# Pooled q, k and v of the first batch summed by TensorE from the blocks' own tiles, with four weight pieces loaded first

## The chip, the cores and the metric

The kernel runs on one core of a Trainium2 chip. The metric is the device time of one execution in microseconds (us); lower is better. The core has TensorE (PE, matrix products), VectorE (DVE), ScalarE (ACT), GpSimd (POOL) and SyncE (SP, which here issues nearly all transfers). PEld is TensorE's loading of the stationary operand.

## The reference

Three layers are computed one after the other. q, k and v are float32 in the shape (batch 4, heads 8, positions 576, depth 64).

```python
def _attn_ref(q, k, v):
    q_d, k_d, v_d = (t.reshape(B, H, 144, 4, D).mean(axis=3) for t in (q, k, v))
    out_up = np.repeat(softmax(q_d @ k_d.T / 8) @ v_d, 4, axis=2)   # pooled attention
    mask = np.abs(pos[:, None] - pos[None, :]) < 4                  # local attention
    out_local = softmax(where(mask, q @ k.T / 8, -1e9)) @ v
    return out_up + out_local            # then as x: 2304 tokens x 512

def _moe_ref(x, w_in, w_out):            # 512 -> 2048 -> 512
    h = x @ w_in
    return (h * np.cos(h)) @ w_out

def _moe2_ref(x, w_gate, w_val, w_out, rms_g):   # 512 -> 1536 -> 512
    xn = x / sqrt(mean(x * x) + 1e-6) * rms_g
    g = xn @ w_gate
    return (silu(g) * (xn @ w_val)) @ w_out
```

## The kernel before, in words

**An order that a planner writes.** The kernel is not written in the order in which it runs. Each piece of work is a Python generator that asks for an engine and a planned duration (`yield "PE", 0.44`), for a buffer (`take`) or for an event (`wait`). The class `Order` steps through them with planned clocks of the engines and emits each instruction to its engine in that planned order. Among pieces that could start within 0.1 us of each other it prefers the one with the earlier due time, weighted by `WD`. Once emitted, each engine runs its own list strictly in order: an instruction that waits holds up all that stand behind it. Where the plan sees PE idle, `keep_warm` puts in products of the identity matrix that nobody uses, named `warm` (line 251).

**The stages.** Attention of a batch has a pooled and a local part. The pooled part needs q and k summed over groups of four positions and transposed (`trq`, line 425 for the first batch), copied into `pqs`; then scores `sps` (line 539), exponentials `E` (line 550), transposes `tra` (line 575), products with pooled v `avp` (line 594), and the result `od` (line 602). The local part goes in five blocks u0 to u4 of about 116 positions: a tile `raw` of 128 positions of q and of k for all heads, transposes `btr` (line 646), scores `bs` (line 690) in a band, exponentials `bE`, transposes `bat` (line 726), products with v `bav` (line 752, with v in `vb`). A block then adds `od` (line 762, DVE), and line 775 (ACT) and line 777 (POOL) split it in two parts into `big`, the input of the first dense layer. That layer works on 256 tokens at a time: `h` (line 1013), cosine (lines 1031 to 1049), `y` (line 1079). The second layer (`gvp`, line 1502, and `o`, line 1755) follows after all of this. The first `h` needs the blocks u0 to u2 of the first batch with their pooled part, and the first weights.

**Weights** come as pieces of 512 KB in a 64-bit format (`raww`), and ACT, DVE and POOL make two TensorE operands of each (lines 316 to 327).

**Before, the start** is made of these transfers, all issued by SP: q and k of the first batch in a layout with the four positions of a group side by side (`pq`, 2.4 MB), with v's blocks (`vb`) in between, four weight pieces, q and k of block u0 once more as `raw`, v in a pooled layout (`v4`, 16 transfers), the blocks u1 to u4. DVE sums q (line 385), POOL sums k (lines 380 and 382) and v (lines 504 to 511).

Of the kernel before, what the change touches and what calls it, by code (L numbers as in the profile page):

```python
# [9 lines left out]
F32 = mybir.dt.float32  # L10
# [37 lines left out]
TP = 5  # L48
WD = 0.005
NQS = 1  # L50
CVB, GLB = 9, 0.5
T0, T1, U1, U2 = 70, 52, 6.5, 4.26
DU = {"conv": 20, "pool": -320, "blk": -200}


class Order:
# [20 lines left out]
    def give(self, name, item, t=None):  # L77
        self.pools.setdefault(name, []).append((self.now() if t is None else t, item))
# [114 lines left out]
def fused_kernel(ctx: ExitStack, tc, q, k, v, w_in, w_out, w_gate, w_val, w_out2, rms_g, mask, bmask, out):  # L193
# [86 lines left out]
    def w_loads(m, pieces, src):  # L280

        for i in pieces:
            S_.due(conv_due(m, i) - 5.0)
            r = yield take("raw")
            p = yield take(PLACES, 1)
# [90 lines left out]
    def sum4(b, w, t, o, n):  # L376

        if b or w:
            yield "POOL", 0.05 + n * 0.32
            POOL.tensor_tensor(out=t[:, :n, 0:2], in0=t[:, :n, 0:2], in1=t[:, :n, 2:4], op=ALU.add)  # L380
            yield "POOL", 0.05 + n * 0.18
            POOL.tensor_tensor(out=o, in0=t[:, :n, 0], in1=t[:, :n, 1], op=ALU.add)
        else:
            yield "DVE", 0.05 + n * 0.27
            DVE.tensor_reduce(out=o, in_=t[:, :n].rearrange("p u r d -> p u d r"), axis=AX.X, op=ALU.add)

# [26 lines left out]

    def pq_first(w, c, t, qs, place):

        u0, n = UC[c]
        yield wait(("pq", w, c))
        yield from sum4(0, w, t, qs[:, u0:u0 + n], n)
        give("pqp", place)
        yield take("att")  # L420
        i = yield take("bank")
        ps = bank_tile(i, [64, 4, 128], "trq")
        yield "PE", 0.2 * n
        for x in range(n):
            PE.transpose(ps[:, x, :], qs[:, u0 + x, :], ident)
        yield from pq_ev(0, w, c, ps)
        give("bank", i)
        give("att", "att")
        count(("pq", 0), 6)

# [55 lines left out]

    def pv(b, hp, t=None, place=None, vh=None):

        vi = 0
        if b == 0:  # L490
            yield wait(("pv", hp))
        else:
            vi = yield take("vh")
            vh = VH[vi]
            p = []
            for _ in range(2):
                x = yield take("pq")
                p.append(x)
            t = (ap.tile([128, 512], F32, tag=p[0], name="v4").rearrange("p (c x) -> p c x", c=2),
                 ap.tile([128, 512], F32, tag=p[1], name="v4")[:, :256])  # L500
            yield from pv_load(b, hp, *t)
# [10 lines left out]
        if b == 0:  # L512
            give(place[2], place)
        else:
            for x in p:
                give("pq", x)
        vd[b, hp] = (vh, vi)
        done(("v", b, hp))

    def pooled(b, hp, E=None):  # L520
# [109 lines left out]
    def block(b, u, raw, pools):  # L630
# [9 lines left out]
        for w in range(2):  # L640
# [4 lines left out]
            for a in range(4):  # L645
                PE.transpose(t[:, a, :], raw[w][:, 2 * a:2 * a + 2].rearrange("t h d -> t (h d)"), ident)  # L646
            if pools[w]:
                give(*pools[w])
# [104 lines left out]
        give("b2", a_i)  # L753
        give("vb", v_i)
        t0 = (S_.cur["t"], "PE")
# [38 lines left out]
    def raw_dma(t, src, b, u):  # L794

        r0 = geo(u)[2]
        yield "SP", 0.73
        SP.dma_start(t, src[b, :, r0:r0 + 128, :].rearrange("h t d -> t h d"))

    VI = {}  # L800

    def block_v():

        for b in range(B):
            for u in range(5):
                S_.due(blk_due(b, u) - 5.0)
                x = yield take("vb")
                VI[b, u] = x
                r0 = geo(u)[2]
                vp = v[b].rearrange("(a e) t d -> e t a d", e=2)  # L810
                for s, (_, _, kc) in enumerate(groups(u)):
                    for e in range(2):
                        yield "SP", 0.5
                        SP.dma_start(VB[x][64 * e:64 * e + 64, s], vp[e, r0 + kc:r0 + kc + 64])
                done(("rv", b, u))

# [25 lines left out]
    def start():  # L842

        pl = {}
        pq_tiles(0)
        for n in [("pq", w, c) for c in range(3) for w in range(2)] + [("qs", w) for w in range(2)] + [("E", hp) for hp in (1, 2, 3)] \
                + [("v4", hp) for hp in range(4)] + [("vhl", 0)] + [("raw", u) for u in range(5)]:
            pl[n] = yield take(PLACES)
# [3 lines left out]

        def load(ev, us):
            yield "SP", us

        qs = [early(("qs", w), [128, 9, 64]) for w in range(2)]
        for c, (u0, n) in enumerate(UC):
            for w in range(2):
                t = early(("pq", w, c), [128, 4, 4, 64])
                yield "SP", max(0.48, 0.37 * n)  # L860
                SP.dma_start(t[:, :n], pq_src(0, w, u0, n))
                done(("pq", w, c))
                S_.add(pq_first(w, c, t, qs[w], pl["pq", w, c]), 0.0, S_.now())
        E = EP + [early(("E", hp), [72, 2, 3, 2, 64]) for hp in (1, 2, 3)]
# [4 lines left out]
        for hp in range(4):  # L869
            S_.add(pooled(0, hp, E[hp]), 0.0)  # L870
        vh0 = early(("vhl", 0), [128, 2, 3, 128])
        vh0 = VH + [vh0[:, 0], vh0[:, 1]]
        for x in vh0:
            yield "POOL", 0.5
            POOL.memset(x, 0.0)
# [12 lines left out]

        def values0():
            for hp in range(4):  # L890
                t = early(("v4", hp), [128, 768])
                t = t[:, :512].rearrange("p (c x) -> p c x", c=2), t[:, 512:]
                yield from pv_load(0, hp, *t)
                done(("pv", hp))
                S_.add(pv(0, hp, t, pl["v4", hp], vh0[hp]), 0.0, S_.now())

# [5 lines left out]

        def raws(us):
            for u in us:
                t = early(("raw", u), [128, 2, 8, 64])
                for w in range(2):
                    yield from raw_dma(t[:, w], (q, k)[w], 0, u)
                done(("raw", 0, u))
                S_.add(block(0, u, (t[:, 0], t[:, 1]), (None, (pl["raw", u][2], pl["raw", u]))), blk_due(0, u))

        first = 0
        for what, n in LOADS:
            if what == "r":
                yield from raws(range(first, first + n))
                first += n
            elif what == "w":
                yield from words(n)
            else:
                yield from values0()
        yield "SP", 0.96  # L920
# [4 lines left out]

        S_.add(after("vhl", None, pl["vhl", 0]), 0.0)
        S_.add(after(("pq", 0), None, pl["qs", 0], pl["qs", 1]), 0.0)
# [5 lines left out]
        yield wait(("E2", 2))  # L933
        for _ in range(3):
            p = yield take("pqp")
            give(p[2], p)

# [910 lines left out]
```

## Time and profile before

| | us |
|---|---|
| median of 3 runs (lowest, highest) | 983.98 (982.58, 985.17) |
| the profiled execution: its time | 984.96 |
| the profiled execution: its span in the trace | 983.1 |
| outside the span | 1.86 |
| first `h` product starts at | 69.87 |
| last stretch, from 200 us to the end | 783.10 |

The span is the time from the first to the last instruction that the profiler saw; the device time of the same execution is 1.86 us longer. TensorE's granted clock is full in all 40 slices of the page.

### The profile page before, as it was taken

To read this page: it belongs to the slowest core of one execution; us is meant where nothing else is said; L and a number is where in the kernel's file an instruction comes from. 1 tells how busy PE (TensorE), PEld (TensorE's weight loads), DVE (VectorE), ACT (ScalarE), POOL (GpSimd) and SP (SyncE) were. 2 spreads that over 40 slices of the span, in tenths; PEclk is the share of its full clock that TensorE was granted. 3 is DMA by queue.
4 is the path that set the end of the run, shared out by engine and by line. 5 is a ranking of instruction groups with operands and counts; after the bars stand their busy time and mean duration, and the time that the engine had idled before them with its cause. 6 is when DMAs were issued, how large, how long until landed. Compare 5 with 4: busy or idle time off the path is not lost.

```text
span 983.1 us, 19205 instructions
## 1 busy us (share of the span) xinstructions
PE 953.0 (97%) x7150; PEld 880.4 (90%) x7150; DVE 721.2 (73%) x1460; ACT 542.3 (55%) x1090; POOL 269.1 (27%) x325
## 2 busy tenths in 40 slices
PE   6789899999999999999999999999999999999998
PEld 6688778888988888888888889999999999999998
DVE  2789976677657775666577699586666688999895
ACT  3658886677677965656566465242322334554442
POOL 3877685544336311101042242000000014300000
PEclk9999999999999999999999999999999999999999
DMA  8788643567685554544331311133222144454432
GB/s 241 212 211 246 181 147 111 148 199 180 199 231 166 170 171 128 176 144 169 120 129 65 107 44 49 49 106 93 75 82 71 57 145 132 132 174 139 141 119 76
DMA packets 160333, 136.07 MB, mean 138 GB/s; under 512 B 72176, under 2 KB 133744, under 8 KB 160240
## 3 DMA queue, kind: packets, MB, share of 16 engines
q1 hardware_dynamic: 160240, 134.85, 45.8%
q8 instruction: 56, 0.92, 0.4%
q14 instruction: 37, 0.30, 0.1%
HBM read 98.64 MB, written 36.18 MB: 137 GB/s over the span
## 4 chain that ended last, share of the span: by engine, by line
PE 84%; DMA 4%; DVE 3%; SPq 3%; issue 2%; POOL 2%; ACT 2%; DVEq 0%; POOLq 0%; ACTq 0%
PE gvp L1502 26%; PE y L1079 19%; PE h L1013 18%; PE o L1755 13%; PE bav L752 2%; PE btr L646 1%; DMA pq<-in_q 1%; DMA raw<-in_k 1%; PE avp L594 1%; PE bs L690 1%; PE yt L1407 1%; POOL wwa L327 1%; PE bat L726 1%; PE sps L539 1%; DMA cst<-in_moe_rms_g 1%
## 5 line engine op out<-in xcount | busy, mean ns | idle before, releaser
L1502 PE MATMUL gvp<-xc,wc 128*128 128x384 f32 x1296 | 231.7, 335 | 0.0
L1502 PEld LDWEIGHTS gvp<-xc,wc 128*128 128x128 f32 x1296 | 225.6, 188 | 0.3
L1573 DVE TENSOR_TENSOR tmp<-gvp,tmp 128x384 f32<-128x384 f32 x180 | 99.3, 553 | 54.3 <-PE gvp L1502 51.0
L1013 PE MATMUL h<-big,wwa 128*128 128x256 f32 (+1 forms) x756 | 124.0, 316 | 0.9 <-DVE t L1038 0.5
L1755 PE MATMUL o<-wo,wc 128*128 128x256 f32 x972 | 118.4, 279 | 0.0
L1013 PEld LDWEIGHTS h<-big,wwa 128*128 128x128 f32 x756 | 107.5, 190 | 10.7 <-DVE t L1038 0.6
L1755 PEld LDWEIGHTS o<-wo,wc 128*128 128x128 f32 x972 | 115.7, 190 | 0.0
L1079 PE MATMUL y<-wwa,big 128*128 128x512 f32 x432 | 109.5, 397 | 0.7 <-DVE big L1049 0.7
L1079 PEld LDWEIGHTS y<-wwa,big 128*128 128x128 f32 x432 | 78.9, 188 | 17.7 <-DVE big L1049 1.6
L1013 PE MATMUL h<-big,wwb 128*128 128x256 f32 (+1 forms) x504 | 83.9, 317 | 0.4 <-DVE t L1038 0.3
L1079 PE MATMUL y<-wwb,big 128*128 128x512 f32 x324 | 82.0, 398 | 1.1 <-POOL big L1049 1.1
L1033 DVE SCALAR_TENSOR_TENSOR t<-kk,h 128x512 f32<-128x512 int32 x72 | 49.0, 681 | 44.1 <-ACT kk L1031 43.9
L1013 PEld LDWEIGHTS h<-big,wwb 128*128 128x128 f32 x504 | 72.0, 190 | 7.8 <-DVE t L1038 0.8
L1031 ACT ACTIVATE kk<-h 128x512 int32<-128x512 f32 x72 | 42.6, 592 | 58.1 <-PE h L1013 55.8
L1079 PEld LDWEIGHTS y<-wwb,big 128*128 128x128 f32 x324 | 59.0, 188 | 13.3 <-POOL big L1049 1.4
L1639 POOL TENSOR_TENSOR wt<-wo 128x256 f32<-128x256 f32 x10 | 9.8, 985 | 208.6 <-DVE wc L1358 183.4
L1038 DVE TENSOR_TENSOR t<-h,t 128x512 f32<-128x512 f32 x72 | 49.3, 686 | 17.9 <-ACT t L1036 17.4
L1564 ACT ACTIVATE tmp<-gvp 128x384 f32<-128x384 f32 x36 | 17.7, 492 | 75.8 <-PE gvp L1502 75.8
L1036 ACT ACTIVATE t<-t,cst 128x512 f32<-128x512 f32 x72 | 51.9, 722 | 13.4 <-DVE t L1033 12.9
L1047 ACT ACTIVATE big<-t 128x512 fp32r<-128x512 f32 x72 | 45.1, 628 | 25.1 <-DVE t L1038 23.7
L1698 ACT ACTIVATE wc<-ut 128x512 fp32r<-128x512 f32 (+1 forms) x60 | 34.3, 584 | 42.2 <-DVE ut L1684 25.3
L1049 DVE TENSOR_TENSOR big<-t,big 128x512 fp32r<-128x512 f32 x54 | 39.8, 738 | 16.6 <-ACT big L1047 16.3
(189 smaller groups left out, 1741.2 us busy)
## 6 DMA issues: line engine op xcount, KB each, us to landing
us<-tmp SPq DMA_DIRECT2D x72, 192.0 KB, 2.0
uf<-us SPq DMA_DIRECT2D x48, 256.0 KB, 3.0
rawwa<-in_moe_w_out SPq DMA_DIRECT2D x21, 512.0 KB, 4.3
wfs<-rawwa SPq DMA_DIRECT2D x36, 256.0 KB, 2.4
rawwa<-in_moe_w_gate SPq DMA_DIRECT2D x12, 512.0 KB, 4.3
rawwa<-in_moe_w_val SPq DMA_DIRECT2D x12, 512.0 KB, 4.6
wf<-wfs SPq DMA_DIRECT2D x12, 512.0 KB, 4.1
vb<-in_v SPq DMA_DIRECT2D x80, 64.0 KB, 2.8
```

What stands on the lines that cost most here:

```text
L1013: PE.matmul(h[:, w_ * ci:w_ * ci + w_], a[:, ksl], x_at(x, kk), start=m == 0, stop=m == 11)
L1031: ACT.activation(out=kk, in_=h, func=ACTF.Copy, scale=INV2PI, bias=0.25)
L1033: DVE.scalar_tensor_tensor(out=t, in0=kk, scalar=TWOPI, in1=h, op0=ALU.mult, op1=ALU.subtract)
L1036: ACT.activation(out=t, in_=t, func=ACTF.Sin, scale=-1.0, bias=cst[:, 0:1])
L1038: DVE.tensor_tensor(out=t, in0=h, in1=t, op=ALU.mult)
L1047: ACT.activation(out=gh, in_=t, func=ACTF.Copy)
L1049: (POOL if e == "POOL" else DVE).tensor_tensor(out=gl, in0=t, in1=gh, op=ALU.subtract)
L1079: PE.matmul(y[j][b], g[:, tsl], a, start=(first and ci == 0 and i == 0), stop=(last and c == 15 and i == 2))
L1502: PE.matmul(bank, w[:, a, kk], xc[:, x, b, kk], start=first and i == 0, stop=i == 5, skip_group_check=True)
L1573: DVE.tensor_tensor(out=half(o), in0=a, in1=half(b), op=ALU.add)
L1698: ACT.activation(out=o[:, 0], in_=src, func=ACTF.Copy)
L1755: PE.matmul(b[m][1][:, l], u[0][x][:, j, l], w[:, y, k], start=(p == 0 and l == 0 and i == 0), stop=(p == C3 - 1 and i == 2), skip_group_c ...
```

## The change: what it does

In short: the sums over four positions for the first batch are made by TensorE, as products with a matrix `sel` of zeros and ones. The separate loads `pq` of the first batch are gone, as are `v4`, the sums of DVE and POOL for this batch, and the transposes `trq` of this batch. In their place:

- `select` fills `sel` at the start from the identity (one POOL instruction, ten of DVE).
- `sums` takes a block's tile of q or k (128 positions by 8 heads by 64) and makes four products with 128 rows and 29 columns; the result is summed and already transposed. One copy by ACT or DVE puts it into `pqs`. There are ten such groups.
- `vsums` makes twelve products with 256 columns from the five blocks' `vb` into two banks, then two copies into `vs`. `avp` of the first batch is now six products of half the array in place of three of the whole one, for each of the four head pairs.
- All five blocks' v are loaded before the next weights, and two more `vb` tiles exist for that.
- Transfers are in a new order: four weight pieces, then the blocks' q on SP; the blocks' k are issued by ACT (line 922 of the changed kernel); then v in 20 transfers; then the next four weight pieces.
- The planner's constants are new.

```diff
-BD = (-80, -45)
+BD = (-40, -45)
-LOADS = (("w", 4), ("r", 1), ("v", 0), ("r", 1), ("w", 4), ("r", 3))
+LOADS = (("w", 4), ("r", 5), ("v", 5), ("w", 4),)
-WD = 0.005
+WD = 0.004
...
+    def sums(u, raw):
...
+        for w in range(2):
...
+            for a in range(4):
+                PE.matmul(ps[:, a, :m], raw[w][:, 2 * a:2 * a + 2].rearrange("t h d -> t (h d)"), M["q"][:, f, j:j + m],
+                          start=a == 0, stop=a == 3, skip_group_check=True)
...
+    def vsums(vs):
...
+        for u in range(5):
+            yield wait(("rv", 0, u))
...
+                    PE.matmul(ps[c // 2][1][:, c % 2], M["v"][:, f, x:x + 128], VB[VI[0, u]][:, s],
+                              start=c // 2 not in seen, stop=False, skip_group_check=True)
...
         for c in range(3):
-            PE.matmul(o, vh[:, c], A[:, c], start=c == 0, stop=c == 2)
+            if b:
+                PE.matmul(o, vh[:, c], A[:, c], start=c == 0, stop=c == 2)
+                continue
+            for e in range(2):
+                pr = slice(64 * e, 64 * e + 64)
+                PE.matmul(o[pr], vh[pr, c, hp], A[pr, c], start=c == 0, stop=c == 2)
...
-                SP.dma_start(t[:, :n], pq_src(0, w, u0, n))
...
+        def load_k(t, u):
+            yield "ACT", 0.3
+            ACT.dma_start(t, k[0, :, geo(u)[2]:geo(u)[2] + 128, :].rearrange("h t d -> t h d"))
```

SP's list at its start, before; each row is one transfer, or several alike, with its destination and source:

```order
L861 DMA pq_109<-in_q 128x1024
L814 DMA vb<-in_v 64x4x64 x4
L861 DMA pq_111<-in_k 128x1024
L814 DMA vb<-in_v 64x4x64 x4
L861 DMA pq_117<-in_q 128x1024
L814 DMA vb<-in_v 64x4x64 x4
L861 DMA pq_140<-in_k 128x1024
L861 DMA pq_167<-in_q 128x256
L861 DMA pq_183<-in_k 128x256
L879 DMA bf<-band_mask 64x144 x2
L291 DMA rawwb_267<-in_moe_w_in 128x4x256
```

The same place of the changed kernel, with the waits of each transfer for an earlier one that had the same semaphore:

```order
L950 DMA bf_128<-band_mask 64x144 x2
L293 DMA rawwa14_137<-in_moe_w_in 128x4x256
L295 DMA rawwa15_139<-in_moe_w_out 128x1024
L293 DMA rawwa16_141<-in_moe_w_in 128x4x256
L295 DMA rawwb0_146<-in_moe_w_out 128x1024
L861 DMA raw0_148<-in_q 128x8x64
L861 DMA raw1_157<-in_q 128x8x64
L861 DMA raw2_167<-in_q 128x8x64 [waits DMAHW1_49]
L861 DMA raw3_255<-in_q 128x8x64 [waits DMAHW2_49]
L861 DMA raw4_309<-in_q 128x8x64 [waits DMAHW4_49]
L873 DMA vb_98<-in_v 64x4x64 [waits DMAHW5_49]
L873 DMA vb_98<-in_v 64x4x64 [waits DMAHW7_49]
```

The weights stand where the pooled q and k stood, and the blocks' tiles right behind them. ACT's list of the changed kernel from its seventh work instruction, where the blocks' k are issued among the conversions of the first weights (`rawwa`, `wwa`) and the copies of the sums:

```order
L322 ACTIVATE rawwa14_137<-rawwa14_137 128x512 [waits DMAHW2_49]
L922 DMA raw0_148<-in_k 128x8x64
L326 ACTIVATE wwa17_143<-rawwa14_137 128x512 [waits DVE_49]
L322 ACTIVATE rawwa15_139<-rawwa15_139 128x512 [waits DMAHW3_49]
L922 DMA raw1_157<-in_k 128x8x64
...
L922 DMA raw2_167<-in_k 128x8x64 [waits DMAHW6_49]
...
L922 DMA raw3_255<-in_k 128x8x64 [waits DMAHW7_49]
...
L922 DMA raw4_309<-in_k 128x8x64 [waits DMAHW4_49]
```

In the kernel before, ACT issued no transfer here. PE's list of the changed kernel in the middle of the start, from the sums of block u3 to the first pooled scores:

```order
L426 MATMUL pq<-sel,raw_255 128x29 x4
L253 MATMUL warm<-ident 128x128 x2
L426 MATMUL pq<-sel,raw_255 128x29 x4
L253 MATMUL warm<-ident 128x128
L786 MATMUL bat<-ident,bE 128x128 x4
L704 MATMUL btr<-ident,raw_167 128x128 x4
L253 MATMUL warm<-ident 128x128
L426 MATMUL pq<-sel,raw_309 128x28 x4
L253 MATMUL warm<-ident 128x128
L704 MATMUL btr<-ident,raw_167 128x128 x4
L426 MATMUL pq<-sel,raw_309 128x28 x4
```

Here `raw_255` is block u3's tile and `raw_309` that of u4, q in the first group and k in the second. Before, PE's list had the pooled scores ahead of all of the blocks:

```order
L425 MATMUL trq<-ident,qs_108 64x128 x4
L251 MATMUL warm<-ident 128x128 x5
L425 MATMUL trq<-ident,qs_108 64x128
L539 MATMUL sps<-pqs 72x144 x16
L646 MATMUL btr<-ident,raw_295 128x128 x4
```

Now the pooled scores stand behind the sums of all five blocks.

## Rows read from the trace of the kernel before

**Rows 1.** The page: TensorE's busy time, and the chain that ended last by engine

```profile
PE 953.0 (97%) x7150; PEld 880.4 (90%) x7150; DVE 721.2 (73%) x1460; ACT 542.3 (55%) x1090; POOL 269.1 (27%) x325
...
PE 84%; DMA 4%; DVE 3%; SPq 3%; issue 2%; POOL 2%; ACT 2%; DVEq 0%; POOLq 0%; ACTq 0%
```

**Rows 2.** Busy us by stretch: PE, PEld, DVE, ACT, POOL; granted clock, DMA share, GB/s

```profile
0.00:20.00 20.00, 13.33 (x99) 12.73 (x100) 4.39 (x3) 4.66 (x11) 6.45 (x15) 1.00 0.78 225
20.00:69.87 49.87, 39.16 (x540) 35.51 (x538) 37.28 (x82) 31.84 (x90) 38.49 (x52) 1.00 0.82 223
69.87:200.00 130.13, 122.59 (x1075) 108.78 (x1075) 101.86 (x179) 96.98 (x186) 82.60 (x94) 1.00 0.59 169
200.00:983.10 783.10, 777.90 (x5443) 723.42 (x5441) 577.62 (x1197) 408.84 (x806) 141.61 (x167) 1.00 0.41 126
```

**Rows 3.** The same stretches, line 251 (warm products) alone: PE, PEld

```profile
0.00:20.00 20.00, 11.69 (x82) 11.27 (x83) 1.00 0.78 225
20.00:69.87 49.87, 18.54 (x136) 16.40 (x134) 1.00 0.82 223
69.87:200.00 130.13, 7.86 (x58) 6.76 (x57) 1.00 0.59 169
```

**Rows 4.** PE's timeline to the first `h`: start, us, group, [idle before <-releaser]

```profile
1.36 3.73 PE L251 MATMUL warm<-ident 128*128 128x128 f32 x16 [1.36 <-POOL cst L233]
...
7.08 3.07 PE L251 MATMUL warm<-ident 128*128 128x128 f32 x26
...
15.68 0.60 PE L425 MATMUL trq<-ident,qs 128*64 128x128 f32 x4 [2.46 <-DVE qs L385]
...
21.69 2.48 PE L539 MATMUL sps<-pqs 64*72 64x144 f32 x32 [0.37 <-ACT pqs L401]
...
66.44 1.14 PE L752 MATMUL bav<-bt,vb 64*64 64x58 f32 x32
...
69.87 1.73 PE L1013 MATMUL h<-big,wwa 128*128 128x256 f32 x12
```

**Rows 5.** Timelines of DVE and of SP's queue: the first pooled load, issue times

```profile
4.68 1.89 DVE L385 TENSOR_REDUCE qs<-pq 128x256 f32<-128x1024 f32 x1 [4.68 <-DMA pq<-in_q]
...
0.73 0.39 SPq L861 DMA_DIRECT2D pq<-in_q  x1
1.18 2.70 SPq L814 DMA_DIRECT2D vb<-in_v  x4
...
38.22 3.60 SPq L436 DMA_DIRECT2D pq<-in_q  x1
```

**Rows 6.** Windows as in rows 2, where weights, then blocks' tiles are under way

```profile
18.00:22.00 4.00, 3.63 (x33) 3.20 (x31) 0.00 (x0) 1.99 (x7) 4.00 (x9) 1.00 1.05 392
23.00:24.00 1.00, 1.00 (x18) 0.90 (x14) 1.00 (x4) 0.99 (x6) 0.08 (x1) 1.00 1.31 223
```

**Rows 7.** Groups by line from 20 to 75 us: busy us, mean ns, idle before

```profile
L655 ACT ACTIVATE bt<-btr 128x512 f32<-128x512 f32 x8 | 4.7, 608 | 3.9 <-PE btr L646 3.9
L550 ACT ACTIVATE E<-sps,stat 72x144 f32<-72x144 f32 x16 | 5.8, 387 | 0.0
L582 ACT ACTIVATE at<-tra 128x288 f32<-128x288 f32 (+1 forms) x7 | 2.2, 353 | 0.1
L762 DVE TENSOR_TENSOR bt<-bav,od 64x464 f32<-64x464 f32 x6 | 3.8, 638 | 2.5 <-PE bav L752 2.4
L777 POOL TENSOR_TENSOR big<-bt,big 128x464 fp32r<-128x464 f32 (+2 forms) x4 | 4.4, 1092 | 3.4 <-ACT big L775 3.4
```

**Rows 8.** Timeline from 178 to 188 us: the weight that came last, and PE

```profile
178.58 0.55 SPq L293 DMA_DIRECT2D rawwa<-in_moe_w_out  x1
...
182.91 0.68 ACT L320 ACTIVATE rawwa<-rawwa 128x512 f32<-128x512 f32 x1 [3.79 <-DMA rawwa<-in_moe_w_out]
...
185.10 1.16 PE L251 MATMUL bs<-ident 128*128 128x128 f32 x8
...
187.60 2.66 PE L1013 MATMUL h<-big,wwa 128*128 128x256 f32 x20 [0.48 <-DVE t L1038]
```

More of the change, by code (lines that the diff above doesn't have):

```diff
@@ L376, in sum4 @@
     def sum4(b, w, t, o, n):
[L378 to L385, printed above, removed]
+        yield "POOL", 0.05 + n * 0.32
+        POOL.tensor_tensor(out=t[:, :n, 0:2], in0=t[:, :n, 0:2], in1=t[:, :n, 2:4], op=ALU.add)
+        yield "POOL", 0.05 + n * 0.18
+        POOL.tensor_tensor(out=o, in0=t[:, :n, 0], in1=t[:, :n, 1], op=ALU.add)
     def pq_src(b, w, u0, n):
@@ L412, in count @@
             done(ev, XT[ev])
[L414 to L429, printed above, removed]
+    M = {}
@@ new lines, in sums @@
+    def sums(u, raw):
+        _, n, _, off = geo(u)
+        m, f, j = n // 4, *{0: (0, 0), 3: (1, 0), 16: (0, 4)}[off]
+        yield wait(("raw", 0, u))
+        yield wait("sel")
+        for w in range(2):
+            yield take("att")
+            i = yield take("bank")
+            ps = bank_tile(i, [128, 4, 29], "pq")
+            yield "PE", 0.5
+            for a in range(4):
+                PE.matmul(ps[:, a, :m], raw[w][:, 2 * a:2 * a + 2].rearrange("t h d -> t (h d)"), M["q"][:, f, j:j + m],
+                          start=a == 0, stop=a == 3, skip_group_check=True)
+            t0 = (S_.cur["t"], "PE")
+            o, sc = PQ[0][w][:, :, 29 * u:29 * u + m], (2.0 ** -7, 1.0)[w]
+            _, e = yield [("ACT", 0.22, t0), ("DVE", 0.2, t0, None, 0.3)]
+            if e == "ACT":
+                ACT.activation(out=o, in_=ps[:, :, :m], func=ACTF.Copy, scale=sc)
+            else:
+                DVE.tensor_scalar(out=o, in0=ps[:, :, :m], scalar1=sc, scalar2=None, op0=ALU.mult)
+            give("bank", i)
+            give("att", "att")
+            done(("pq0", u, w))
+            count(("pq", 0), 10)
@@ new lines, in fused_kernel @@
+    VW = ((0, 0, 15), (2, 15, 29), (1, 29, 44), (2, 44, 58), (1, 58, 73), (2, 73, 87), (1, 87, 102), (2, 102, 116), (1, 116, 131), (3, 131, 144))
+    def vsums(vs):
+        ps = []
+        for c in range(2):
+            yield take("att", 1 - c)
+            i = yield take("bank")
+            ps.append((i, bank_tile(i, [128, 2, 4, 64], "pv")))
+        seen = set()
+        for u in range(5):
+            yield wait(("rv", 0, u))
+            yield "PE", 1.1
+            for s in range(2):
+                f, p0, p1 = VW[2 * u + s]
+                for c in sorted({p0 // 48, (p1 - 1) // 48}):
+                    x = 47 - (p0 - 48 * c)
+                    PE.matmul(ps[c // 2][1][:, c % 2], M["v"][:, f, x:x + 128], VB[VI[0, u]][:, s],
+                              start=c // 2 not in seen, stop=False, skip_group_check=True)
+                    seen.add(c // 2)
+        t0 = (S_.cur["t"], "PE")
+        for c in range(2):
+            n = 2 - c
+            _, e = yield [("ACT", 0.1 + 0.26 * n, t0), ("DVE", 0.1 + 0.29 * n, t0, None, 0.3)]
+            o = vs[:, 2 * c:2 * c + n]
+            if e == "ACT":
+                ACT.activation(out=o, in_=ps[c][1][:, :n], func=ACTF.Copy)
+            else:
+                DVE.tensor_copy(out=o, in_=ps[c][1][:, :n])
+            give("bank", ps[c][0])
+            give("att", "att")
+        for hp in range(4):
+            vd[0, hp] = (vs, None)
+            done(("v", 0, hp))
@@ new lines, in select @@
+    def select(t):
+        M["q"] = t[:, 0:64].rearrange("p (f x) -> p f x", f=2)
+        M["v"] = t[:, 64:832].rearrange("p (f x) -> p f x", f=4)
+        yield "POOL", 0.8
+        POOL.memset(t[:, 0:832], 0.0)
+        yield "DVE", 1.5
+        for f, (a, n) in enumerate(((0, 32), (3, 31))):
+            DVE.tensor_reduce(out=M["q"][:, f, 0:n], in_=ident[:, a:a + 4 * n].rearrange("p (x r) -> p x r", r=4), axis=AX.X, op=ALU.add)
+        for f, (a, n) in enumerate(((0, 15), (3, 15), (5, 14), (12, 13))):
+            for e in range(2):
+                DVE.tensor_reduce(out=M["v"][:, f, 47 + 64 * e:47 + 64 * e + n], in_=ident[:, 64 * e + a:64 * e + a + 4 * n].rearrange("p (x r) -> p x r", r=4),
+                                  axis=AX.X, op=ALU.add)
+        done("sel")
@@ L485, in pv_load, with pv @@
                 SP.dma_start(tb[64 * e + n:64 * e + 64], flat(v, f0 * 64, [[256, 64 - n], [1, 256]]))
[L487 to L501, printed above, removed]
+    def pv(b, hp):
+        vi = yield take("vh")
+        vh = VH[vi]
+        p = []
+        for _ in range(2):
+            x = yield take("pq")
+            p.append(x)
+        t = (ap.tile([128, 512], F32, tag=p[0], name="v4").rearrange("p (c x) -> p c x", c=2),
+             ap.tile([128, 512], F32, tag=p[1], name="v4")[:, :256])
+        yield from pv_load(b, hp, *t)
         ta, tb = t[0].rearrange("p c (r d) -> p c r d", r=4), t[1].rearrange("p (r d) -> p r d", r=4)
@@ L511, in pv @@
             POOL.tensor_tensor(out=vh[pr, 2, 64 * e:64 * e + 64], in0=tb[pr, 0], in1=tb[pr, 1], op=ALU.add)
[L512 to L516, printed above, removed]
+        for x in p:
+            give("pq", x)
         vd[b, hp] = (vh, vi)
@@ L593, in pooled @@
         for c in range(3):
-            PE.matmul(o, vh[:, c], A[:, c], start=c == 0, stop=c == 2)
+            if b:
+                PE.matmul(o, vh[:, c], A[:, c], start=c == 0, stop=c == 2)
+                continue
+            for e in range(2):
+                pr = slice(64 * e, 64 * e + 64)
+                PE.matmul(o[pr], vh[pr, c, hp], A[pr, c], start=c == 0, stop=c == 2)
         give(a, x)
@@ L646, in block @@
                 PE.transpose(t[:, a, :], raw[w][:, 2 * a:2 * a + 2].rearrange("t h d -> t (h d)"), ident)
+            if not b:
+                yield wait(("pq0", u, w))
             if pools[w]:
@@ L753, in block @@
         give("b2", a_i)
-        give("vb", v_i)
+        if v_i < NV:
+            give("vb", v_i)
+        else:
+            count("vb0", 2)
         t0 = (S_.cur["t"], "PE")
@@ L796, in raw_dma, with load_v @@
         r0 = geo(u)[2]
-        yield "SP", 0.73
+        yield "SP", 1.75
         SP.dma_start(t, src[b, :, r0:r0 + 128, :].rearrange("h t d -> t h d"))
     VI = {}
+    def load_v(b, u, x):
+        VI[b, u] = x
+        r0 = geo(u)[2]
+        vp = v[b].rearrange("(a e) t d -> e t a d", e=2)
+        for s, (_, _, kc) in enumerate(groups(u)):
+            for e in range(2):
+                yield "SP", 0.5
+                SP.dma_start(VB[x][64 * e:64 * e + 64, s], vp[e, r0 + kc:r0 + kc + 64])
+        done(("rv", b, u))
     def block_v():
-        for b in range(B):
+        yield wait(("rv", 0, 4))
+        for b in range(1, B):
             for u in range(5):
@@ L807, in block_v @@
                 x = yield take("vb")
[L808 to L815, printed above, removed]
+                yield from load_v(b, u, x)
     def blk_due(b, u):
@@ L845, in start @@
         pq_tiles(0)
[L846 to L847 removed]
+        for n in [("raw", u) for u in range(5)] + ["sel", "vb", "vs"] + [("E", hp) for hp in (1, 2, 3)] + [("E2", x) for x in range(3)]:
             pl[n] = yield take(PLACES)
@@ L851, in early, with raws @@
             return pl[n][0].tile(shape, dtype, tag=pl[n][1], name="".join(map(str, n)))
[L853 to L860, printed above, removed]
-                SP.dma_start(t[:, :n], pq_src(0, w, u0, n))
-                done(("pq", w, c))
-                S_.add(pq_first(w, c, t, qs[w], pl["pq", w, c]), 0.0, S_.now())
+        def load_k(t, u):
+            yield "ACT", 0.3
+            ACT.dma_start(t, k[0, :, geo(u)[2]:geo(u)[2] + 128, :].rearrange("h t d -> t h d"))
+        def raws(us):
+            for u in us:
+                t = early(("raw", u), [128, 2, H, D])
+                S_.add(load_k(t[:, 1], u), 0.0, 0.0)
+                yield "SP", RAWT
+                yield from raw_dma(t[:, 0], q, 0, u)
+                done(("raw", 0, u))
+                S_.add(sums(u, (t[:, 0], t[:, 1])), SD, S_.now())
+                S_.add(block(0, u, (t[:, 0], t[:, 1]), (None, (pl["raw", u][2], pl["raw", u]))), blk_due(0, u), S_.now())
+        S_.add(select(early("sel", [128, 1024])), -60)
+        for x in range(3):
+            give("pqp", pl["E2", x])
         E = EP + [early(("E", hp), [72, 2, 3, 2, 64]) for hp in (1, 2, 3)]
@@ L869, in start @@
         for hp in range(4):
[L870 to L873, printed above, removed]
+            S_.add(pooled(0, hp, E[hp]), PD)
+        for x in VH:
             yield "POOL", 0.5
@@ L887, in start, with values0 @@
         done("mask")
[L889 to L895, printed above, removed]
+        vbx = early("vb", [128, 2, 2, 4, 64])
+        VB.extend(vbx[:, x] for x in range(2))
+        def values0(us):
+            for u in us:
+                x = NV + u - 3
+                if u < 3:
+                    x = yield take("vb")
+                yield from load_v(0, u, x)
+                if u == 0:
+                    S_.add(vsums(early("vs", [128, 3, 4, 64])), VD, S_.now())
         nw = [0]
@@ L901, in words @@
             yield from w_loads(1, range(i, nw[0]), w1_src)
[L903 to L911, printed above, removed]
+        first = {"r": 0, "v": 0}
         for what, n in LOADS:
[L913 to L916, printed above, removed]
+            if what == "w":
                 yield from words(n)
-            else:
-                yield from values0()
+                continue
+            i = first[what]
+            first[what] += n
+            yield from (raws if what == "r" else values0)(range(i, i + n))
         yield "SP", 0.96
@@ L932, in start @@
             S_.add(free_E2(x), 0.0)
[L933 to L936, printed above, removed]
     def free_E2(x):
```

11 lines of the change are left out of this document (7 added, 4 removed).

## The prediction, made before the changed kernel had run

> **What bounds the kernel.** I began with the page: TensorE is busy for 97% of the span, and the chain of work that ended last is TensorE's for 84% [rows 1]. So time can be won only where TensorE waits or runs warm products. The windows by stretch show where that is. To the first h product at 69.87 us TensorE is busy 13.33 + 39.16 = 52.5 us [rows 2], of which 11.69 + 18.54 = 30.2 us are warm products [rows 3]. That is 22.3 us of work in 69.9 us, so 47.6 us of this start are idle or warm. From 69.87 to 200 us it is 130.13 - 122.59 = 7.5 us idle and 7.9 us warm, 15.4 us in all. From 200 us on only 5.2 us are idle [rows 2]. The change works in the start. **What counts is when the first h starts**, and then whether the second stretch, whose weights and attention of the next batches run beside it, can follow.
>
> **What the start costs now.** Until 21.69 us TensorE only transposes pooled q and k and runs warm; then the pooled scores stand in one block of 2.48 us [rows 4]. The first pooled load was issued at 0.73 and landed at 4.68 us; v's 64 KB transfers cost the queue 2.70/4 = 0.68 us each to issue [rows 5]. The blocks follow only then: the last `bav` before h starts at 66.44 [rows 4].
>
> **A. The new loads.** The two band transfers go first, so the first weight is issued at about 1.9 us and lands, by the 4.0 us of the first pooled load [rows 5], at 5.9. Weights moved at 392 GB/s [rows 6], so 512 KB take 1.3 of these 4.0 us and 2.6 lie ahead of the data. Four are 2.10 MB, 5.4 us of moving from 4.5 on: the last lands at about 10. Then q of five blocks and k of three are 8 x 256 KB = 2.10 MB. While the blocks' tiles, whose pieces are 256 bytes long, were under way, the rate was 223 GB/s [rows 6]: 9.4 us, to 19.4. k of u3 stands in ACT's list behind a wait for an earlier transfer on its semaphore, the second of v, which lands at some 20.5. Issue, the 2.6 us ahead of the data and 1.2 us for 256 KB give 25 to 25.5. k of u4 waits in the same way for the seventh of v (23.5) and **lands at about 28**. Bounds: 24, if only the bytes count (2.6 MB and 0.5 MB of v at 223 GB/s from 10 us); 31, if the 20 transfers of v take half of the rate.
>
> That ACT's issues add no bandwidth is my assumption, since the trace of before has no transfer issued by ACT here. The Trainium skill says the same ("DMA: Bandwidth & Descriptors", "Issuing engines are not separate DMA queues"): transfers of any engine run on the same 16 DMA engines, and only issue time is saved. Were it otherwise, k of u0 to u2 would come beside q and the raws end some 3.5 us sooner.
>
> **B. From there to pooled v.** Nothing in the trace is a product with 29 columns in float32. Its nearest row is the warm product: 3.07/26 = 0.118 us a record with 128 columns, two records a product [rows 4]. A group of four has 8 records, so 0.94 us; if columns alone counted, 0.25. I take 0.94, since the 128 rows of weights are loaded as for the warm product. The twelve products for v have 256 columns, four times 0.118 = 0.47 each, 5.6 in all (bounds 0.24 and 0.94 each, so 2.9 and 11.3). Between the last sum and the last of these stand the pooled scores 2.48, a block's scores (32 records of about the columns that `bav` has, 1.14 for 32 [rows 4]) and three groups of four transposes, four records or 0.47 each: together 0.94 + 5.6 + 2.5 + 1.1 + 1.4 = 11.5. **39.5 us.** ACT's 16 exponentials of 5.8 us [rows 7] begin when the first scores are there, near 31, and end at 37: covered by the products for v.
>
> **C. ACT to the last pooled result.** From the copy of v sums to the fourth `od` ACT's list has eight operations of 128 by 512 at 0.608, seven `at` at 0.353, four `od` and the copy at about 0.387 (rows of the same width) [rows 7]: 4.9 + 2.5 + 1.9 = 9.3 us. Starts follow up to 0.1 us sooner than durations add, which takes 2 off, and four waits for TensorE put 1.5 on: 9 (bounds 7.4 and 11). **48.5 us.** TensorE's own part in it, 24 half-array products with 144 columns, is by the warm record 24 x 2 x 0.118 x 144/128 = 6.4 us at most and lies beside ACT.
>
> **D. To the first h.** `bav` of three blocks follows at 1.14 us each; the first is ready 1 us on, DVE's two additions 2 x 0.638, ACT's copy 0.5, then POOL's part of u0, u1 and a corner of u2, 1.2 + 1.2 + 0.6 by 1.092 for the mean piece, and two sums of 0.6 of the next batch between [rows 4, 7]: 7.5, so 56. DVE and POOL share the weights' conversions here; I add 2. **First h at 58 us, 11.9 sooner** (bounds 50 and 65 with all ends together). The added work of TensorE ahead of it, 9.4 for the sums and 5.7 for v, costs nothing, since 47.6 us were idle or warm; without that cover it would cost 15. The first 8 weights are four sooner than needed: only the order of the loads, not a rate, decides them.
>
> **E. Behind the first h.** `bat` and `bav` of u3 now stand ahead of it, 0.47 + 1.14 less 0.47 for a group of transposes that moved behind: -1.1 us. **F.** At 182.91 ACT gets a weight that SP issued at 178.58 behind v's transfers, and TensorE runs 1.16 us warm and waits 0.48 [rows 8]. In the new list the last weight of this layer stands ahead of those transfers: -1.6. **G.** With h 12 us sooner the weights and the next batch's blocks are asked for sooner, out of the same queue: I give back 1.5 of it (bounds 0 to 12).
>
> **The sum.** 984.96 - 11.9 - 1.1 - 1.6 + 1.5 = 971.9 by the profiled execution, which lies 1 us over the median of the runs: **972 us**. Its own range is 965 to 979, from first h 52 to 64.
>
> **The rivals.**
>
> 1. **The clock falls (slower).** For some 5 us, until k of u3 lands, TensorE stands before that product with nothing to run; its longest wait ahead of h is now 2.46 us [rows 4]. The warm products at 1.36 us took 3.73/16 = 0.233 us, those at 7.08 half of it [rows 4]: the ratio of its two levels, 1.2 and 2.4 GHz, though the granted clock of the stretch reads 1.00 [rows 2]. If it fell to the lower one there and stayed to the first h, some 27 us of work would take twice as long; with part of that hidden by ACT, I put 16 us: first h at 74 and 988 us. In all later stretches too the granted clock is 1.00, so no row shows a fall behind work. If it fell for a moment only, it costs 1.8 us (16 records at twice the time). It decides if the first h is beyond 73. Chance 6%. The Trainium skill ("TensorE: Matmul & The Clock Gate", Part 1, the HAM clock gate) speaks for it: an idle array is put to half its clock until it has worked steadily again.
>
> 2. **ACT is held up by its own issues (slower).** A transfer's issue took 0.39 to 3.60 us on SP [rows 5]. At 3.60 each, five would hold ACT's conversions and copies by 15 us more, and everything of B to D lies behind it: first h at 73, 987 us. Half of that gives 979. The full price: 5%.
>
> 3. **The second stretch gives it back (same).** If weights and v of the next batch can't come sooner, the 15.4 us idle or warm from the first h to 200 become some 25: 982 us. DVE is busy 101.86 of 130.13 there and the queues 0.59 [rows 2], so neither is full. Chance 13%.
>
> 4. **It gains there too.** With eight weights early and u3 done, the 15.4 us halve: 964 us. Chance 15%.
>
> My forecast has the remaining 59%, and 2% go to what I haven't seen, on the slower side. A measurement can tell from no change about 0.3%, 3 us: faster (below 981) is 59 + 15 = 74%, same 13%, slower 6 + 5 + 2 = 13%. The range is 963 to 985: beyond it lie most of rivals 1 and 2 (11%) and the low end of rival 4 (6%).
>
> **What would show it.** Right: a first h (now line 1076) near 58 us; k of u3 and u4 landing at 25 and 28, with TensorE's longest wait before the sums of u3; ACT's list running without gaps from v's copy to the last `od`; 14 to 18 us idle or warm in the 130 us behind the first h, and no wait for the last weight. Wrong: a granted clock below 1.00 between 18 and 60 us; products of 29 or 256 columns at twice my price; POOL or DVE, not ACT, last ahead of `od`; or a first h at 58 and a total that has not moved, with new warm products from 70 to 200 us.

## The result and the profile after

The changed kernel takes 975.49 us (median of 5 runs, 974.16 to 975.93) against 983.98 before; the ratio is 0.991 with a 95% interval of 0.9895 to 0.9924. So it is faster by 0.9%. The forecast was 972 with a range of 963 to 985.

The page of the changed kernel, its busy times and its chain by engine; these answer to [rows 1]:

```profile
PE 957.8 (98%) x7194; PEld 884.3 (91%) x7194; DVE 719.7 (74%) x1459; ACT 542.8 (56%) x1091; POOL 254.1 (26%) x301
...
PE 84%; DVE 9%; ACT 2%; SPq 2%; issue 2%; DMA 1%; DVEq 0%; ACTq 0%
```

DVE has 9% of the chain, where it had 3%. The windows by stretch, cut at the new start of the first h and 130 us behind it; first all work, which answers to [rows 2], then warm products alone, as [rows 3]:

```profile
0.00:20.00 20.00, 18.64 (x178) 18.44 (x178) 8.76 (x21) 8.23 (x17) 8.79 (x17) 1.00 1.01 223
20.00:62.75 42.75, 40.17 (x542) 35.24 (x542) 31.54 (x75) 25.77 (x79) 15.43 (x16) 0.96 0.51 143
62.75:192.90 130.15, 123.09 (x1019) 109.63 (x1016) 95.93 (x158) 99.14 (x186) 87.55 (x98) 0.99 0.58 166
...
0.00:20.00 20.00, 14.28 (x106) 13.75 (x106) 1.00 1.01 223
20.00:62.75 42.75, 7.56 (x50) 6.29 (x50) 0.96 0.51 143
62.75:192.90 130.15, 7.70 (x50) 6.80 (x50) 0.99 0.58 166
```

The first h starts at 62.75 us, 7.1 sooner; the span is 973.8, 9.3 shorter, so the rest is 2.2 us shorter. From 20 us to the first h, idle and warm time is 2.6 + 7.6 = 10.1 us, where it was 29.3. The 130 us behind the first h have 7.1 us idle and 7.7 warm: 14.8, where they had 15.4. The granted clock, 1.00 before in every stretch, is 0.96 and 0.99 in two of them.

TensorE's timeline answers to [rows 4]:

```profile
1.36 12.59 PE L253 MATMUL warm<-ident 128*128 128x128 f32 x96 [1.36 <-POOL ident masks.py:199]
13.79 0.97 PE L426 MATMUL pq<-sel,raw 128*128 128x29 f32 x8
...
31.19 0.97 PE L426 MATMUL pq<-sel,raw 128*128 128x28 f32 x8
...
41.74 1.03 PE L458 MATMUL pv<-vb,sel 128*128 128x256 f32 x4
...
50.26 0.95 PE L652 MATMUL avp<-at,vs 64*64 64x144 f32 x12 [1.09 <-ACT at L635]
51.94 1.17 PE L652 MATMUL avp<-at,vs 64*64 64x144 f32 x12 [0.73 <-DVE at L637]
...
62.75 4.87 PE L1076 MATMUL h<-big,wwa 128*128 128x256 f32 x36
```

From 13.79 to 42.8 us TensorE has no wait above 0.3 us: it is the bound there, with 34 warm records among its work before 31.19. Behind the two waits at 50 us and another of 2.32 us at 73 the granted clock falls. Four windows, with TensorE's busy time first and the clock third from the end:

```profile
51.00:52.00 1.00, 0.27 (x6) 0.06 (x4) 0.96 (x4) 0.02 (x1) 0.29 (x1) 1.00 0.00 0
53.00:54.00 1.00, 1.00 (x12) 0.73 (x14) 0.88 (x3) 1.00 (x3) 0.00 (x0) 0.50 0.00 0
57.00:58.00 1.00, 1.00 (x42) 1.00 (x38) 0.94 (x3) 0.20 (x1) 0.57 (x1) 1.00 0.23 53
73.00:74.00 1.00, 0.86 (x16) 0.86 (x18) 1.00 (x3) 1.00 (x3) 0.92 (x2) 0.51 1.19 224
```

0.50 is the lower of the two levels, 1.2 GHz; each fall lasted some 3 us. This is one execution: run 8 below has the same list up to some 300 us and the same waits, and its profile shows no fall.

The queues, from the timelines of SP and ACT, and SP's last three issues of q by themselves, from the chain of waits:

```profile
4.20 10.50 SPq L861 DMA_DIRECT2D raw<-in_q  x5
14.75 17.80 SPq L873 DMA_DIRECT2D vb<-in_v  x20
...
22.22 0.40 ACTq L922 DMA_DIRECT2D raw<-in_k  x1
22.72 0.67 ACT L326 ACTIVATE wwa<-rawwb 128x512 fp32r<-128x512 f32 x1 [5.08 <-DMA vb<-in_v]
...
5.79 4.20 SPq L861
10.04 1.62 SPq L861
11.70 3.00 SPq L861
```

SP needs 10.5 us for five issues, and 8.8 of them for the last three. Each of these three has a wait for an earlier transfer on its semaphore, but that is not what held it: by the trace the awaited transfers had landed at 3.4, 5.9 and 8.8 us, before the issues began at 5.8, 10.0 and 11.7. So the issues themselves were long, while transfers issued before them were still under way; why is not shown. ACT does wait for a semaphore: it stands 5.1 us before the fourth k, until a v transfer has landed.

The longest pieces of the chain of waits from 39 to 53 us (start, us, what):

```profile
39.53 1.53 DVE stat L597 x4
...
48.58 1.00 DVE rawwb L318 x3
...
50.21 1.12 DVE bst L769
...
51.94 1.17 PE avp L652 x12
```

From 39.53 to 51.89 every piece of it is DVE's.

### The profile page after: what moved, and what is told of

It is laid out like the page before. It is cut to its first block, busy times and chain, and to the rows that moved or that the text cites. A ratio compares the mean times of both kernels' runs of the same rounds, so it can differ in the third digit from the quotient of the medians.

```text
span 973.8 us, 19223 instructions
## 1 busy us (share of the span) xinstructions
PE 957.8 (98%) x7194; PEld 884.3 (91%) x7194; DVE 719.7 (74%) x1459; ACT 542.8 (56%) x1091; POOL 254.1 (26%) x301
## 4 chain that ended last, share of the span: by engine, by line
PE 84%; DVE 9%; ACT 2%; SPq 2%; issue 2%; DMA 1%; DVEq 0%; ACTq 0%
PE gvp L1565 26%; PE y L1142 18%; PE h L1076 16%; PE o L1818 13%; PE bav L812 2%; PE btr L704 1%; SPq L861 1%; PE bs L750 1%; PE yt L1470 1%; PE avp L648 1%; DVE rawwa L324 1%; PE sps L592 1%; DMA rawwa<-in_moe_w_out 1%; DVE bt L825 1%; PE bat L786 1%
## 5 line engine op out<-in xcount | busy, mean ns | idle before, releaser
L1672 DVE TENSOR_TENSOR tmp<-tmp 128x384 f32<-128x384 f32 x72 | 43.7, 608 | 11.9 <-ACT tmp L1660 11.4
```

Of the source, the lines that this page charges most:

```text
L1672: DVE.tensor_tensor(out=half(v), in0=half(v), in1=half(sl), op=ALU.mult)
```

## Experiments

Every ratio is to the kernel before, timed in the same rounds. Where an experiment's interval overlaps that of the changed kernel, its time doesn't tell the two apart, and its profile, which is one execution, is read.

**1. k issued by SP.** All other lists are the same.

```diff
-            ACT.dma_start(t, k[0, :, ...])
+            SP.dma_start(t, k[0, :, ...])
```

> The blocks' k are issued by SP, each just ahead of its q, in place of ACT; every other engine's list is the same. Theory 1 (ACT was held: its list stood from 17.7 to 22.2 us before the issue of the fourth k, which waits for the second v transfer, and TensorE then waits for ACT's copies): the last k lands near 22 us and not near 28, ACT's idle 5.1 us ahead of the fourth weight's copy goes, first h 59 to 60 us in place of 62.75, total 972 to 973. Rival 1 (two issuing queues were worth something): SP is held by the same waits, v comes later, first h 62 to 65, total 975 to 978.

974.7 us, ratio 0.9912 (0.9899 to 0.9925): by time not told from the changed kernel. ACT's wait is gone, the first h starts at 61.78 with the clock at 1.00 throughout. The chain shows why it is no more: it runs through TensorE from its first instruction. TensorE's timeline follows, with the same two waits at 50 us as in the changed kernel:

```profile
1.36 13.62 PE warm L253 x96
14.97 0.81 PE pq L426 x8
...
14.81 0.97 PE L426 MATMUL pq<-sel,raw 128*128 128x29 f32 x8
...
50.79 0.95 PE L652 MATMUL avp<-at,vs 64*64 64x144 f32 x12 [1.09 <-ACT at L635]
52.46 0.95 PE L652 MATMUL avp<-at,vs 64*64 64x144 f32 x12 [0.72 <-DVE at L637]
...
61.78 0.38 PE L1076 MATMUL h<-big,wwa 128*128 128x256 f32 x1
```

A caution for all first h that follow: the opening warm products took 13.62 us here and 12.59 in the changed kernel, so the sums begin at 14.81 and not at 13.79; over the profiles with 96 such records they begin anywhere from 13.7 to 15.0. It is safer to count from the first sums: the first h comes 47.0 us behind them here, 49.0 in the changed kernel's profile, and 47.0 in run 8, where ACT issues k and the clock stays at 1.00 too (15.02 to 62.02). Of these 2.0 us the fall of the clock costs 1.5: from the last `avp` to the first h it is 10.8 us in the changed kernel's profile and 9.3 here and in run 8. The other 0.5 lie between the first sums and the last v product (29.0, and 28.5 here and in run 8).

Theory 1 falls: ACT's wait cost at most these 0.5 us, and nothing where the sums began later (run 8), because TensorE had work until then. SP's late v (issued from 19.52 to 34.1 us) cost nothing either.

**2. All five k issued by ACT at once.**

```diff
-                S_.add(load_k(t[:, 1], u), 0.0, 0.0)
+            for u, t in zip(us, ts):          # ahead of the loop over q
+                ACT.dma_start(t[:, 1], k[0, :, ...])
```

> All five k are issued by ACT one behind the other after its first conversion, none behind a v transfer. Theory 1 (as above): the last k lands at 20 to 23 us, ACT waits early (7 to 15 us) where nobody needs it, first h 59 to 60, total 972 to 973. Rival 2 (TensorE itself, with its warm products in between, is the bound from 24 to 39 us): the k come sooner and nothing moves, first h 62, total 975.

987.45 us, ratio 1.0039 (1.0006 to 1.0073): 12 us slower than the changed kernel by the medians. Neither expectation held. The median stands between two groups: six of the twelve executions took 981 to 983 us, six 991 to 997. The profiled one took 992.56 and belongs to the second; what the first six looked like inside is not shown. Timelines of ACT's queue and of TensorE, and windows by 10 us:

```profile
6.23 11.29 ACTq L927 DMA_DIRECT2D raw<-in_k  x5
...
24.83 1.13 PE L750 MATMUL bs<-bt 64*64 64x64 f32 x32 [5.70 <-ACT bt L715]
25.89 1.91 PE L426 MATMUL pq<-sel,raw 128*128 128x29 f32 x8
...
20.00:30.00 10.00, 5.17 (x51) 5.05 (x52) 5.72 (x10) 5.45 (x12) 3.88 (x3) 0.62 0.68 120
40.00:50.00 10.00, 10.00 (x49) 10.00 (x49) 1.75 (x4) 3.10 (x7) 0.00 (x0) 0.50 0.47 162
50.00:60.00 10.00, 10.00 (x90) 7.34 (x89) 5.65 (x16) 5.89 (x25) 1.29 (x2) 0.84 0.01 3
```

The issues hold ACT from 6.2 to 17.5 us: 5.5 us are the five issues, 5.7 us waits between them for earlier transfers to land. The copies of the first sums and transposes come late, TensorE waits 5.70 us, and its clock falls to 1.2 GHz and stays there until some 53 us: a group of sums takes 1.91 in place of 0.97 us. The first h starts at 80.2. In this execution these are rivals 1 and 2 of the prediction in one: the first h is 17 us later than in the changed kernel, where each had been given 15 to 16.

**3. No warm products between 10 and 60 us of the plan.**

```diff
-        if n < 1 or t0 > FT2 or ...
+        if n < 1 or 10 < t0 < 60 or t0 > FT2 or ...
```

> No warm products between 10 and 60 us of the plan (the 48 at the start stay); all else is in the same order. Theory 2 (TensorE is on the path from 24 to 39.5 us, and 1.7 us of that path are warm products): first h 61 to 61.7, total 973.5 to 974.5. Rival: the warm products keep the clock: without them the granted clock falls before 40 us, first h 64 or later, total 977 or more.

979.52 us, ratio 0.996 (0.9948 to 0.9972): slower than the changed kernel by 4 us. The rival held. TensorE's timeline:

```profile
23.42 0.38 PE L744 MATMUL bs<-bm,ident_r 128*128 128x256 f32 x1 [0.97 <-ACT pqs L432]
...
24.83 5.32 PE L426 MATMUL pq<-sel,raw 128*128 128x29 f32 x24
```

Its work comes to 23.4 us sooner, waits for a copy, and the clock falls: three groups take 5.32 us. In the windows the granted clock is 0.72 from 20 to 30 us and 0.50 from 30 to 40; the first h starts at 68.7.

**4. All normalisations of E on POOL.**

```diff
-            (POOL if e == "POOL" else DVE).tensor_tensor(out=x, ...
+            (POOL if e == "POOL" or not b else DVE).tensor_tensor(out=x, ...
```

> All eight normalisations of the first batch's E are POOL's; four of them were DVE's (2.9 us). Theory 3 (DVE's list is the path from 39.5 to 51.9 us, not ACT's, as the prediction had it): first h 60.3 to 61, total 973 to 974. Rival (ACT's list is the path, or POOL's part slows DVE by as much): first h 62.5 to 63, total 975 to 976.

974.23 us, ratio 0.9906 (0.9891 to 0.9921): by time not told from the changed kernel. In the profile the first h starts at 60.31, as theory 3 says, and the clock stays at 1.00. But 1.5 of the 2.4 us are the clock's. What the edit gave is 1.2 us: from the last v product's end to the last `avp` it is 8.0 us, in place of 9.2 in the changed kernel and in runs 1 and 8. So DVE was on the path, but it got back less than the 2.9 us of the four operations. One of its conversions now took long while POOL worked beside it; by its timeline:

```profile
41.82 1.88 DVE L318 TENSOR_SCALAR rawwb<-rawwb 128x512 int32<-128x512 int32 x1
```

The same operation took 0.42 us in the changed kernel. That POOL's work was the cause is likely, but no run tests it.

**5. Blocks and v first, then the weights.**

```diff
-LOADS = (("w", 4), ("r", 5), ("v", 5), ("w", 4),)
+LOADS = (("r", 5), ("v", 5), ("w", 8),)
```

> The loads are in the order blocks, v, eight weights; the four weights no longer come first. Theory 2 (from the first sums on, TensorE works without a gap, so that its start sets its end): the first sums start at 8 to 10 us in place of 13.8, the last v product ends near 37 in place of 42.7; then DVE and ACT have all eight weights to convert in 27 to 60 us, where the four first ones were done by 17 us before: 4 to 5 us of DVE back. First h 60 to 64, total 973 to 977. Rival (loading weights first costs the blocks 5 us and gives nothing): first h 57 to 58, total 970 to 971. Other rival (the waits of ACT's issues make TensorE idle and its clock falls): total above 980.

996.09 us, ratio 1.0125 (1.0106 to 1.0144): the slowest of all, though its first h is the earliest. Timelines of TensorE, SP's queue and DVE, and a window:

```profile
56.52 0.39 PE L1076 MATMUL h<-big,wwa 128*128 128x256 f32 x1
...
73.56 0.43 SPq L293 DMA_DIRECT2D rawwb<-in_moe_w_in  x1
...
77.65 0.43 DVE L318 TENSOR_SCALAR rawwb<-rawwb 128x512 int32<-128x512 int32 x1 [4.90 <-DMA rawwb<-in_moe_w_in]
...
60.00:80.00 20.00, 17.29 (x173) 16.02 (x172) 12.52 (x18) 11.98 (x23) 12.45 (x14) 0.91 0.75 196
```

The first sums start at 9.05 and v's products end at 38, as theory 2 says. What makes it slow stood in no expectation: the planner's list now has six weights ahead of the next batch's loads in place of ten, and the ninth is issued at 73.56, behind loads that wait for POOL and TensorE. DVE stands 4.90 us for it, and TensorE fills with warm products and idles. **An early first h is worth nothing where the weights don't follow**: my measure of the change was only half of it.

**6, 7, 8. The constants.** The changed kernel with all three old constants; with the weight of the due times alone put back; with the later blocks' due time alone. The edits, written in short form (the three constants stand on lines of their own):

```diff
-BD, WD, DU["blk"] = (-40, -45), 0.004, -170
+BD, WD, DU["blk"] = (-80, -45), 0.005, -200   # 6: all; 7: WD alone; 8: DU["blk"] alone
```

> The changed kernel with the planner's three old constants (block due times -80 and -200, weight 0.005). If the gain is that of the new sums and loads, as I think: 974 to 978. If the constants carry it: 980 or more.

> The changed kernel with the due times' weight alone put back to 0.005. The order to 110 us is the same. Theory 6 (the 7 us that the old constants lost lie between 110 and 150 us, in an order where TensorE waits for DVE and its clock then falls; that order comes from this weight): 980 to 983, first h as in the changed kernel. Rival (the block due time did it): 975 to 976.

> The changed kernel with the later blocks' due time alone put back to -200; the order differs only in the later part of the dense layer, behind some 300 us. Theory 6: 975 to 977. Rival: 980 or more.

With all old ones 982.33 us, ratio 0.9985 (0.9971 to 0.9999); with the weight alone 981.72, ratio 0.9973 (0.9959 to 0.9986); with the block due time alone 976.37, ratio 0.9912 (0.9894 to 0.993). So 0.004 against 0.005 is worth about 6 us, and the block time nothing that is measured. The first expectation was wrong: I had given the constants no part. Theory 6 held for the weight. TensorE's timeline with the old weight, and one window of it:

```profile
136.71 1.57 PE L1142 MATMUL y<-wwa,big 128*128 128x512 f32 x5 [2.23 <-DVE big L1112]
...
143.50 0.50 PE L1142 MATMUL y<-wwb,big 128*128 128x512 f32 x1 [1.20 <-ACT big L1110]
...
140.00:150.00 10.00, 8.27 (x37) 6.62 (x37) 5.56 (x11) 7.10 (x12) 8.11 (x9) 0.76 0.29 87
```

The same window of the changed kernel, where the order has more h products in that place:

```profile
140.00:150.00 10.00, 10.00 (x80) 9.12 (x78) 6.09 (x12) 9.62 (x23) 7.44 (x10) 1.00 0.24 68
```

With the old weight TensorE comes to y products before their input is there, waits, and works at a lower clock behind each wait. Its first h had started at 61.0 us, sooner than in the changed kernel's profile by what the clock cost there.

**9. The new constants alone in the kernel before.**

> The kernel before with the three new constants alone (block due times -40 and -170, weight 0.004); sums and loads as they were. Theory 5 (the constants fit the order behind the new start and are worth nothing by themselves): 981 to 990, first h near 70. Rival (the constants carry some 7 us in either kernel, and the new start 1 to 2): 976 to 978.

988.42 us, ratio 1.0042 (1.0026 to 1.0059): slower than before by 0.4%. Theory 5 held for the time, though its first h is not near 70. TensorE's timeline has a new wait, and the granted clock is 0.91 from 20 to 60 us:

```profile
23.86 1.09 PE L646 MATMUL btr<-ident,raw 128*128 128x128 f32 x4 [6.93 <-DMA raw<-in_q]
```

Its first h starts at 65.7, 4 us sooner than before, and it is slower all the same. New sums and loads alone give 0.15%, new constants alone lose 0.4%, both together gain 0.9%.

**10. Gaps filled with warm products.** 4 and 2 ahead of the last two `avp`, 8 ahead of `bav` of u4.

> The changed kernel with 4, 2 and 8 more warm products where TensorE stood for 1.1 and 0.7 us ahead of the last two pooled products and 2.3 us ahead of the last block's product with v, each time with its granted clock at half behind it. Theory 4 (the two falls of the clock cost some 1.5 us each where they show): the granted clock is 1.00 in all stretches, first h 61 to 62, total 973 to 974 with a smaller spread. Rival (TensorE isn't the path there, or the falls are rare): 975 to 976.

974.4 us, ratio 0.9904 (0.9886 to 0.9922): not told from the changed kernel by time (973.2 to 977.1, no narrower). In the profile the clock is 1.00 in all stretches, and the first h starts at 61.6, 47.0 us behind the first sums. But the profiles of runs 1, 6 and 8 have the waits unfilled (1.1, 0.7 and 2.3 us), no fall before 100 us and the same 47.0. So neither that the filling kept the clock up nor that it pays is shown.

**11, 12. All together,** with 40 and with 48 warm products at the start.

> k issued by SP, the normalisations by POOL, the gaps filled as in the run beside, and 40 warm products in place of 48 ahead of the first sums. If the three theories (ACT's wait 1 us, DVE's list 2.4 us, the clock 1 to 1.5 us) add up and TensorE's first products start 1 to 2 us sooner: first h 57.5 to 59, total 969.5 to 971.5. Rival: without the 8 warm products TensorE stands ahead of the first sums and its clock falls: 976 or more.

> k issued by SP, the normalisations by POOL and the gaps filled, with all 48 warm products at the start (the run with 40 had its clock fall between 20 and 40 us). If the small gains add up where the clock stays at 1.00: first h 59 to 60, total 970.5 to 972.5. Rival (the second stretch gives part of it back): 973 to 974.

973.08 us, ratio 0.9885 (0.9867 to 0.9903), and 973.1 us, ratio 0.9879 (0.986 to 0.9898). They beat the kernel before; against the changed one they are 0.2 to 0.3% better by these ratios, with intervals that just overlap. Starting the sums 0.9 us sooner (12.88) gained nothing: from 27 to 31 us the clock fell there. With all 48, the first h starts at 60.38, no sooner than in run 4:

```profile
60.38 4.98 PE L1080 MATMUL h<-big,wwa 128*128 128x256 f32 x36
```

That is 2.4 us sooner than in the changed kernel, but 1.5 of them are the clock's there: it comes 46.7 us behind the first sums, against 47.0 in runs 1 and 8 and 46.0 in run 4. So the theories didn't add up.

## Why the prediction was right, point by point

**What bounds the kernel.** That time could be won in the start held. That the first h then decides did not: runs 5 and 9 start it sooner and lose, and run 7, whose list is the same up to there, loses behind it. The total followed the first h only because the list behind it fitted.

**A, the loads.** k of u3 was issued at 22.22 and of u4 at 23.99 us, behind v's transfers, as foreseen. By the trace they landed at 25.5 and 29.5, where I had 25 to 25.5 and 28, and TensorE has no wait for either. I had not seen that SP itself would be held, 10.5 us for five issues.

**B, sums and v.** The prices were right: 0.81 to 0.97 us a group (0.94; by columns alone it would have been 0.21, not the 0.25 that I wrote), some 0.45 a product for v (0.47). From the last group's start to the last v product took 31.2 to 42.8 = 11.6 us (11.5). The step that failed is its start: I took TensorE as free when u4's k lands, at 28, but it was busy from 13.8 us on with the other sums, the blocks and 34 warm records, and came to that group 3.2 us later. That the k itself landed 1.5 us late didn't matter: in run 1 it landed at 22.1, by the trace, and TensorE came to the group at 31.7. That the added work "costs nothing" was wrong by these 3.2 us.

**C, to the last pooled result.** 42.8 to 53.7 = 10.9 us, not 9, and DVE's list, not ACT's, was the path (run 4). That is the second step that failed: I had priced ACT alone and never added DVE's copies, normalisations and conversions.

**D.** 53.7 to 62.75 = 9.1 us (9.5; the terms that I listed add up to 7.1 and not to 7.5, before the 2 for conversions). It includes a fall of the clock: 51.94 to the first addition of DVE took 4.5 us, and 3.0 in run 1 at full clock, so about 1.5 us.

**E to G.** The rest is 2.2 us shorter (1.2 forecast). F's mechanism was right: the last weight of this layer is issued at 155.29, ahead of the `vb` transfers that it stood behind before, and nothing waits for it. The sizes of E, F and G don't show one by one; if E and F came as priced, G gave back 0.5 in place of 1.5. And that holds only with the new weight of the due times: with the old one 6 us more are lost, inside the bound of 12. No term of my sum priced the constants, so that they kept the gain was luck as far as the prediction goes.

**The sum.** 4.8 us of the first h's 11.9 didn't come (3.3 in B with its start, 1.9 in C, less 0.4 in D), and the rest gave 1 us more: the span shrank by 9.3 us where 13.1 were forecast, and 975.5 lies inside the likeliest case's own range. The time was right and the path half wrong: of my signs of being wrong two came, a granted clock below 1.00 between 18 and 60 us and DVE, not ACT, last ahead of `od`.

**The rivals.** Rival 1 happened in small: the clock fell twice for 3 us, at places I hadn't named, while the 5 us wait for k of u3 didn't come. Runs 2 and 3 show the full one. The Trainium skill's rule ("TensorE: Matmul & The Clock Gate", Part 1, the HAM clock gate) says that an idle array is put to half its clock until it has worked steadily again; gaps of 1 to 7 us stood ahead of the falls shown here, but for one in run 11; the same gaps stood without a fall in the profiles of runs 1, 6 and 8, so the trace agrees only in part. Rival 2 was one of order: ACT's issues cost 0.4 us each, and the wait in front of the fourth cost little here; in run 2 issues and waits held ACT for 11.3 us. Rival 3's mechanism, weights that come too late, is real in run 5. Run 7 loses in the same stretch by waits for DVE and ACT, which the new constants avoided. Rival 4 didn't come: 14.8 of the 15.4 us idle or warm are left.

## What to carry to other kernels

Follow every engine's list to the point that counts, not only that of the engine that you suspect: here TensorE and then DVE were the path where I had ACT and the loads. A gain in the start is kept only if the order behind it has work ready, so retune the planner's constants with the change and time both apart and together. Before you take filler out, or bring work forward, look at what the clock does behind the gap, and in more than one execution: a fall in a single profile can look like the effect of an edit.

## What the runs showed of the hardware that I had not expected

The granted clock stayed at 1.2 GHz for very different times: some 3 us behind the gaps at 50 and 73 us of the changed kernel, and some 30 us in the profiled execution of run 2, where groups of sums with 29 columns followed a wait of 5.70 us. Behind the same gaps (1.1, 0.7 and 2.3 us) it didn't fall at all in the profiles of runs 1, 6 and 8. In run 11 it fell at 27 us with no wait of TensorE in the rows; what came before were such groups and warm products. What tells these apart stays open. SP's issue of a 256 KB transfer took from 0.46 to 4.20 us in the changed kernel, with no semaphore left to wait for. A DVE conversion of 0.42 us took 1.88 us while POOL worked beside it (run 4).
